# Squares of eleven pairs of heads summed by ScalarE in nine accumulating instructions each, and the order of all work computed anew

## The chip, the cores and the metric

One core of a Trainium2 chip runs the whole program. The metric is the time of one execution in device microseconds, as the median of a few runs; lower is better. One execution was also recorded by the hardware profiler; its trace has the start and the length of every instruction. In what follows PE is TensorE, PEld its weight loads, DVE VectorE, ACT ScalarE, POOL GpSimd and SP the engine that issues most DMAs.

## The reference

Linear attention with random features over 8 batches and 8 heads of 576 rows of 64 numbers, then an MLP (SiLU between two matrices) over the 4608 rows that result:

```python
scale = 1.0 / np.sqrt(np.sqrt(D))
q_s, k_s = (q * scale, k * scale)
def phi(x):
    proj = np.einsum('bhsd,md->bhsm', x, omega)
    sq = np.sum(x * x, axis=-1, keepdims=True) / 2.0
    h = proj - sq
    h = h - np.max(h, axis=-1, keepdims=True)
    return np.exp(h) / np.sqrt(m)
q_p, k_p = (phi(q_s), phi(k_s))
kv = np.einsum('bhsm,bhsd->bhmd', k_p, v)
z = np.sum(k_p, axis=2)
num = np.einsum('bhsm,bhmd->bhsd', q_p, kv)
den = np.einsum('bhsm,bhm->bhs', q_p, z)[..., None] + 1e-06
...
h = x @ w_in
g = h * (1.0 / (1.0 + np.exp(-h)))
return g @ w_out
```

The change is at `sq`, the sum of 64 squares of each row of q and k.

## The kernel before

**Pairs.** Two heads of a batch make a pair; there are 32, numbered 0 to 31, each with a key part (k) and a query part (q). Of each part one copy (`rawk`, `rawq`) comes transposed for PE and one (`nat`) with rows on partitions, 128 by 9 columns by 64, for the squares. `square` squares the `nat` tile on ACT in place, in one instruction of 576 elements a partition; `square_sum` adds 64 squares each on DVE into nine numbers (`sqk`, `sqq`). There are two `nat` buffers for all pairs; a buffer is free for the next load when the sum has read it.

**From a pair to its output.** PE projects (`project`, and `project_mid` for the 128 rows that straddle the two heads, called the middle). DVE takes the maximum of each row (`top`) and makes the shift out of maximum and square sum (`shift`, tiles `nbk` and `nbq`). Then one of two routes: *direct*, where ACT computes nine exponentials straight out of PSUM with the shift as bias (`expo`), or *lowered*, where DVE adds the shift in three operations (`lower`) and ACT takes one exponential over all 1152 columns (`expo_all`). `straight(n, who)` decides: direct below pair 8, and from `STRAIGHT_K` or `STRAIGHT_Q` on. Then PE sums the keys (`zsum`, for the first eight pairs `zsum_direct`) and multiplies them with v (`kv`), DVE makes the normalizer (`denom`: nine or ten products with an accumulator and one reciprocal, tile `rd`), POOL multiplies the queries by it (`normal`), PE transposes them (`turn`; ACT copies, tile `en`) and multiplies (`numer`). ACT copies the result out (`x_high`, `x_rest`), DVE makes its low part (`x_low`).

**The MLP.** The first three blocks of 512 rows go through `stage1` (first matrix, bank h or fx), `silu` and `g_low`, and `stage2` (second matrix, bank acc), with every operand in a high and a low part, so three matmuls stand for one. The other rows go through three rounds of a matrix scheme with seven products in place of eight: `product` and `gather` for the first matrix, `whole_silu`, `g_sum`, `g_high` (ACT) and `g_rest` (DVE, the low part) and `second` for the second. PE starts with the pairs alone; the MLP's first steps come in between from about 58 us on, from about 464 us the scheme's rounds share the time with the last pairs, and from 752 us on PE has the MLP alone.

**What sets the order.** All of it stands in a list of units, each with an engine, a booked length, a due time (`key`), the units that must come before it, and the buffers that it takes and frees. `Plan.run` places them one after the other and so fixes the order on every engine; an engine then works strictly in that order and waits by semaphores for the others. The constants at the head (`STAY`, `SLACK`, `SPREAD_*`, `EARLY_SUMS`, `PREPARE_*`, `LEAD_W`) shift due times; each seed in `SHIFTS` moves the due times of a random part of the units. PSUM has eight banks: four acc, one h, one fx, two att, and the plan decides which bank a unit gets. Before the first projection PE is kept warm by matmuls of `ones` (`warm` and `pulses`).

Of the kernel before, what the change touches and what calls it, by code (L numbers as in the profile page):

```python
# [13 lines left out]
AF = mybir.ActivationFunctionType  # L14
# [5 lines left out]
P = 128  # L20
# [16 lines left out]
DIRECT = 8  # L37
STRAIGHT_K = 22.298
STRAIGHT_Q = 24.404
NARROW = 4  # L40
# [14 lines left out]
for _f in range(16):  # L55
# [19 lines left out]
SWITCH = 1.3  # L75
STAY = 19.856
HANDOFF = {"PE": 0.25, "ACT": 0.1, "DVE": 0.1, "POOL": 0.15, "SP": 0.2}
CALM = 0.5
SHIFTS = (
# [3 lines left out]
)  # L83
# [233 lines left out]
def attention_mlp(ctx: ExitStack, tc: tile.TileContext, qT, kT, qn, kn, v, om_in, w_in, w_out, out, out_t):  # L317
# [55 lines left out]
    def square(n, who):  # L373
        nat = T["nat", n, who]
        nc.scalar.activation(nat, nat, AF.Square, scale=SCALE * 0.5**0.5)  # L375

# [639 lines left out]
    for n in range(NWIN):  # L1016
        calm = n < LEAD
        for i, who in enumerate("kq"):
# [3 lines left out]
            def prev(s):  # L1022
                return [(s,) + x for x in last]
# [566 lines left out]
```

## Time and profile before

| | |
|---|---|
| median of 3 runs | 1021.39 us (1021.1 to 1022.64) |
| profiled execution, its own time | 1022.64 us |
| span of its instructions | 1020.8 us |
| mean granted TensorE clock | 0.990 |
| square on ACT, 64 instructions | 44.3 us |
| sum of squares on DVE, 64 instructions | 2 x 23.8 us |
| first MLP matmul | 58.39 us |
| last pair's last product on PE | 750.59 us |
| last matmul ends | 1016.4 us |

The busy time of PE is modelled at the ends of its matmuls, so a busy PE is not a full one. The slices on the page cut the span in 40 parts of 25.5 us; a digit is the busy share in tenths. Of the page's other parts: the chain of work that ended last is PE for 81%, DVE for 10%, ACT for 4% and DMA for 3%, and DVE's part of it lies between 463 us and 719 us and in the first 100 us.

### The profile page before, as it was taken

The page shows a single profiled execution, that of the slowest core. Times are in us where ns is not written, and L with a number is a line of the kernel's source. Part 1 is how long each engine was busy: PE and PEld are TensorE (multiplying, and loading weights), DVE is VectorE, ACT ScalarE, POOL GpSimd, SP SyncE. Part 2 cuts the span into 40 slices and gives each one's busy share as a digit, 9 for nine tenths or more (in the row PEclk, how much of TensorE's full clock was granted, in tenths as well). Part 3 has the DMA queues.
Part 4 walks back from the last instruction along what each step waited for, and adds up shares of the span by engine and source line. Part 5 has one row for each costly group of instructions (what it writes and reads, how often), then busy time and mean ns, then how long its engine had stood idle before and what let it go on. Part 6 is the DMA issues. An engine that isn't in the chain of part 4 may idle for free.

```text
span 1020.8 us, 17425 instructions
## 1 busy us (share of the span) xinstructions
PE 987.1 (97%) x5792; PEld 792.2 (78%) x5792; DVE 786.1 (77%) x1895; ACT 615.5 (60%) x1225; POOL 359.3 (35%) x447
## 2 busy tenths in 40 slices
PE   7879998999999999999999998999999999999997
PEld 6757877777777787787777776877878888888886
DVE  5879888877877787888986699998657984556863
ACT  4678676655566666676879685656635553324541
POOL 1425554466757776575563313230100000000000
PEclk9889999999999999999999999999999999999999
DMA  7676667677776777768888665866555568566564
GB/s 286 209 254 202 217 239 255 219 248 243 227 227 211 248 243 236 243 226 300 291 282 295 207 198 179 306 211 235 195 200 202 188 209 258 193 197 195 189 213 154
DMA packets 107592, 232.94 MB, mean 228 GB/s; under 512 B 14704, under 2 KB 39408, under 8 KB 107504
## 3 DMA queue, kind: packets, MB, share of 16 engines
q1 hardware_dynamic: 107200, 231.52, 68.2%
q8 instruction: 46, 0.75, 0.3%
q10 hardware_dynamic: 304, 0.33, 0.1%
q14 instruction: 42, 0.34, 0.1%
HBM read 182.52 MB, written 49.28 MB: 227 GB/s over the span
## 4 chain that ended last, share of the span: by engine, by line
PE 81%; DVE 10%; ACT 4%; DMA 3%; issue 1%; POOL 0%; POOLq 0%; SPq 0%; DVEq 0%; ACTq 0%
PE ps_acc L822 13%; PE ps_acc L936 12%; PE ps_acc L983 11%; PE ps_h L737 11%; PE ps_att L936 4%; PE ps_att L822 3%; PE ps_fx L936 3%; PE ps_att L402 3%; DVE prod L488 2%; PE ps_h L936 2%; PE ps_fx L822 2%; PE ps_fx L402 2%; PE ps_fx L500 2%; PE ps_att L500 1%; PE ps_fx L737 1%
## 5 line engine op out<-in xcount | busy, mean ns | idle before, releaser
L822 PE MATMUL ps_acc<-w,x 128*128 128x512 f32 x696 | 171.9, 396 | 0.9 <-DVE w L869 0.5
L822 PEld LDWEIGHTS ps_acc<-w,x 128*128 128x128 f32 x696 | 127.9, 188 | 29.1 <-DVE w L869 0.7
L518 POOL TENSOR_TENSOR hq<-hq,rd 128x384 f32<-128x384 f32 x96 | 82.2, 882 | 188.6 <-DVE rd L493 152.2
L737 PE MATMUL ps_h<-x,w 128*128 128x512 f32 x504 | 133.9, 403 | 3.3 <-ACT en L536 2.6
L983 PE MATMUL ps_acc<-wo,gh 128*128 128x512 f32 x384 | 124.6, 405 | 0.0
L737 PEld LDWEIGHTS ps_h<-x,w 128*128 128x128 f32 x504 | 92.1, 190 | 24.4 <-ACT en L536 2.8
L936 PE MATMUL ps_acc<-w,x 128*128 128x512 f32 x360 | 94.1, 394 | 0.4 <-DVE w L926 0.4
L983 PEld LDWEIGHTS ps_acc<-wo,gh 128*128 128x128 f32 x384 | 67.9, 188 | 14.5
L936 PEld LDWEIGHTS ps_acc<-w,x 128*128 128x128 f32 x360 | 66.6, 188 | 15.2 <-DVE w L926 0.9
L983 PE MATMUL ps_acc<-wo,gl 128*128 128x512 f32 x192 | 75.2, 392 | 0.0
L488 DVE CUSTOM_DVE_ANT_0 prod<-hq,ps_att 128x128 f32<-128x128 f32 (+1 forms) x160 | 45.9, 287 | 26.3 <-PE ps_att L508 12.0
L936 PE MATMUL ps_acc<-gh,x 128*128 128x512 f32 x160 | 58.2, 393 | 0.0
L375 ACT ACTIVATE nat<-nat 128x576 f32<-128x576 f32 x64 | 44.3, 696 | 20.7 <-DMA nat<-qn 10.8
L880 DVE TENSOR_TENSOR gl<-gf,gh 128x512 fp32r<-128x512 f32 x48 | 39.5, 825 | 13.9 <-ACT gf L876 13.7
L874 ACT ACTIVATE gh<-ps_h 128x512 fp32r<-128x512 f32 x42 | 25.1, 598 | 37.1 <-PE ps_h L737 34.6
L459 POOL TENSOR_TENSOR t<-hk 128x256 f32<-128x256 f32 x48 | 38.3, 817 | 22.6 <-ACT hk L452 20.4
L983 PEld LDWEIGHTS ps_acc<-wo,gl 128*128 128x128 f32 x192 | 36.0, 188 | 8.0
L536 ACT COPY en<-ps_att 128x384 f32<-128x384 f32 x46 | 21.7, 480 | 33.8 <-PE ps_att L524 30.7
L936 PEld LDWEIGHTS ps_acc<-gh,x 128*128 128x128 f32 x160 | 30.1, 188 | 6.3
L822 PE MATMUL ps_att<-w,x 128*128 128x512 f32 x138 | 34.8, 390 | 0.0
L779 POOL TENSOR_TENSOR wraw<-w,wraw 128x256 fp32r<-128x256 f32 x32 | 24.3, 758 | 27.9 <-ACT wraw L777 27.3
L467 POOL TENSOR_TENSOR es<-es,hk 64x128 f32<-64x128 f32 x48 | 26.4, 549 | 19.2 <-ACT hk L438 16.6
(450 smaller groups left out, 2534.7 us busy)
## 6 DMA issues: line engine op xcount, KB each, us to landing
x<-ws SPq DMA_DIRECT2D x84, 512.0 KB, 4.3
x<-wt SPq DMA_DIRECT2D x48, 512.0 KB, 4.0
x<-wo_d SPq DMA_DIRECT2D x72, 256.0 KB, 3.3
wo<-wo_d SPq DMA_DIRECT2D x32, 512.0 KB, 3.9
rawk<-kT SPq DMA_DIRECT2D x32, 352.0 KB, 4.0
rawq<-qT SPq DMA_DIRECT2D x32, 352.0 KB, 4.7
v<-v SPq DMA_DIRECT2D x32, 320.0 KB, 4.5
nat<-kn SPq DMA_DIRECT2D x32, 288.0 KB, 4.2
```

The source lines that it names most:

```text
L375: nc.scalar.activation(nat, nat, AF.Square, scale=SCALE * 0.5**0.5)
L402: nc.tensor.matmul(ps[:, i * M : (i + 1) * M], raw[r, o : o + P], oms[r], start=True, stop=True)
L459: nc.gpsimd.tensor_tensor(T["t", n][:, part], e[:, 5 * part : 5 * part + 2], e[:, 5 * part + 2 : 5 * part + 4], ALU.add)
L467: nc.gpsimd.tensor_tensor(T["es", n][r, j], T["es", n][r, j], e[r, MID], ALU.add)
L488: nc.vector.tensor_tensor_reduce(out=prod[r], in0=e[r, c], in1=z[r, j * M : (j + 1) * M], scale=1.0, scalar=GUARD, op0=ALU.mult, op1=ALU.a ...
L500: nc.tensor.matmul(ps[j * D : (j + 1) * D, :M], vt[:, c + j], e[:, c], start=i == 0, stop=i == 4)
L518: nc.gpsimd.tensor_tensor(e[:, c], e[:, c], rd[:, c].unsqueeze(2).broadcast_to([P, 3, M]), ALU.mult)
L737: nc.tensor.matmul(ph, w[:, i], x[:, j], start=k == 0 and n == 0, stop=k == NK - 1 and n == 2)
L822: nc.tensor.matmul(ph, ws[:, u, kk * P : (kk + 1) * P], o[:, x], start=i in (0, 1, 4) and kk == 0 and n == 0, stop=kk == 1 and n == 2, ski ...
L880: nc.vector.tensor_tensor(gl, T.pop(("gf", t, f)), T["gh", t, f].bitcast(F32), ALU.subtract)
L936: nc.tensor.matmul(T["qb", p, chain][d], w[:, u, d * P : (d + 1) * P], x, start=i in (0, 1, 4) and s == 0 and n == 0, stop=s == NS - 1 and ...
L983: nc.tensor.matmul(T["po", t][j], g[:, js], w, start=f == 0 and n == 0, stop=f == NF - 1 and n == 2)
```

## The change

The test `summed(n)` picks pairs 22 to 31 (22.000 is the border) and, by its second half, pair 0. For these ACT squares and sums in one: nine instructions of 64 columns, each with an accumulator output that goes into one of the nine numbers. The DVE reduction of these 22 tiles falls away, and the `nat` buffer is free after ACT's ninth. The borders of the direct route move: k from pair 23 on before, from 26 now; q from pair 25 on before, from 24 now. Constants and seeds (40 before, 48 now) are others, and by them the whole order.

```diff
@@ -35,8 +35,10 @@
+SUMMED_FROM = 22.000
+SUMMED_TO = 0.482
-STRAIGHT_K = 22.298
-STRAIGHT_Q = 24.404
+STRAIGHT_K = 25.339
+STRAIGHT_Q = 23.117
...
-STAY = 19.856
+STAY = 17.388
...
-    55, 761, 1230, 1684, 2043, 2652, 3396, 5453, 5899, 6430, 7010, 8410, 8796, 9966, 11076, 11672, 12487,
+    39, 528, 1932, 2796, 3494, 4104, 5306, 6136, 6388, 6984, 7584, 7818, 8321, 8679, 9726, 10682, 11322,
...
-EARLY_SUMS = 18.806
-PREPARE_1 = 22.764
-PREPARE_2 = 2.035
-LEAD_W = 14.593
+EARLY_SUMS = 14.192
+PREPARE_1 = 16.093
+PREPARE_2 = 12.582
+LEAD_W = 13.938
@@ -372,6 +375,12 @@
         nat = T["nat", n, who]
+        if summed(n):
+            T.pop(("nat", n, who))
+            T["sq", n, who] = s = new(f"sq{who}", [P, 10])
+            for c in range(NC):
+                nc.scalar.activation(nat[:, c], nat[:, c], AF.Square, scale=SCALE * 0.5**0.5, accum_out=s[:, c : c + 1])
+            return
         nc.scalar.activation(nat, nat, AF.Square, scale=SCALE * 0.5**0.5)
@@ -1007,6 +1016,9 @@
+    def summed(n):
+        return n >= SUMMED_FROM or n < SUMMED_TO
...
-                add(("sq",) + w, "ACT", 0.7, at(n, 2 * i - 4, 13 + 10 * i - 32), lambda n=n, who=who: square(n, who),
-                    after=[("nat",) + w])
-                add(("ssum",) + w, "DVE", 0.76, at(n, 2 * i - 3, 14 + 10 * i - 32), lambda n=n, who=who: square_sum(n, who),
...
+                wide = summed(n)
+                add(("ssum",) + w if wide else ("sq",) + w, "ACT", 2.3 if wide else 0.7, at(n, 2 * i - 4, 13 + 10 * i - 32), lambda n=n, who=who: square(n, who),
...
+                if not wide:
+                    add(("ssum",) + w, "DVE", 0.76, at(n, 2 * i - 3, 14 + 10 * i - 32), lambda n=n, who=who: square_sum(n, who),
```

In all, 22 ACT instructions of 576 columns become 198 of 64 columns; ACT has 18 direct exponentials fewer and two of 1152 columns more, and two table loads fewer; DVE has 22 reductions fewer and six `lower` operations more; PE has one warming matmul more. POOL and SP have as many instructions as before.

Lines in the new program are some 9 higher in this part (L379 of before has no counterpart, L418 is L427, L477 is L486, L488 is L497, L926 is L935).

**The start, on DVE.** The first rows of DVE's program, before; `sqk` and `sqq` are pair 0's sums, `mxk` and `mxq` its maxima, `nbk` and `nbq` its shifts.

```order
L379 TENSOR_REDUCE sqk<-nat 128x9
L418 TENSOR_REDUCE mxk<-ps_att 128x4
L418 TENSOR_REDUCE mxk<-ps_fx 128x4
L379 TENSOR_REDUCE sqq<-nat 128x9
L416 TENSOR_REDUCE mxk<-ps_acc 128x1
L422 TENSOR_TENSOR nbk<-mxk,sqk 128x9
L423 SCALAR_TENSOR_TENSOR nbk<-nbk,sqk 128x9
```

And now:

```order
L427 TENSOR_REDUCE mxk<-ps_att 128x4
L427 TENSOR_REDUCE mxk<-ps_fx 128x4
L425 TENSOR_REDUCE mxk<-ps_acc 128x1
L431 TENSOR_TENSOR nbk<-mxk,sqk 128x9
L432 SCALAR_TENSOR_TENSOR nbk<-nbk,sqk 128x9
```

The two reductions are gone; the shift of the keys follows the maxima at once. On PE, 17 warming matmuls stand ahead of the first projection in place of 13, and the three ahead of pair 1's projection are gone. Somewhat later PE runs three groups of `stage1` ahead of pair 3's query projection, which stood ahead of them; on DVE the query shift of pair 3 comes behind the one of pair 4, and the normalizers of pairs 3 and 4 follow each other; on ACT the three copies of pair 2's transposes stand ahead of the squares of pair 4, where the third stood behind them.

**Pair 7's key sum, on PE.** Before, from the query middle of pair 7 (L409) over the second stage (L983), the product with v and the output product of pair 6 (L500, L562) to the key sum (L477, L479) and the next `stage1` step (L737):

```order
L409 MATMUL ps_fx<-oms,rawq 128x128
L983 MATMUL ps_acc<-wo,gh 128x512 x2
L983 MATMUL ps_acc<-wo,gl 128x512
L500 MATMUL ps_att<-hk,v 64x128 x10
L562 MATMUL ps_att<-en,kw 64x512 x2
L562 MATMUL ps_att<-en,kw 64x64 x2
L477 MATMUL ps_fx<-hk,sides 128x128
L479 MATMUL ps_fx<-hk,ones 128x128 x4
```

Now, from the end of the `stage1` step (L746) over the middle (L418) and the key sum (L486, L488) to the second stage (L992):

```order
L533 MATMUL ps_att<-ident,hq 128x128 x3
L746 MATMUL ps_h<-x_1079,w_1867 128x512 x3
L418 MATMUL ps_att<-oms,rawq 128x128
L486 MATMUL ps_fx<-hk,sides 128x128
L488 MATMUL ps_fx<-hk,ones 128x128 x4
L486 MATMUL ps_fx<-hk,sides 128x128
L488 MATMUL ps_fx<-hk,ones 128x128 x4
L992 MATMUL ps_acc<-wo,gh 128x512 x2
```

The middle has moved from bank fx to a bank of att, so the key sum no longer takes the bank that the middle's exponential must free. The product with v and the output product (now L509, L571) come after the key sum and four groups of the second stage.

**Pair 27's normalizer, on DVE.** Before, its last read and its reciprocal (L488, L493) with what follows; L926 is `g_rest`, L902 `g_sum`, L418 to L423 maxima and shift of pair 28:

```order
L488 ISA den 128x1
L493 RECIPROCAL rd<-den 128x9
L902 TENSOR_TENSOR x_6025<-w_7062,x_6025 128x512
L926 TENSOR_TENSOR w_7067<-wo,w_7067 128x512
L418 TENSOR_REDUCE mxk<-ps_att 128x4
L902 TENSOR_TENSOR x_6025<-w_7062,x_6025 128x512
L418 TENSOR_REDUCE mxk<-ps_att 128x4
L422 TENSOR_TENSOR nbk<-mxk,sqk 128x2x4
L423 SCALAR_TENSOR_TENSOR nbk<-nbk,sqk 128x2x4
L926 TENSOR_TENSOR gl<-wo,gh 128x512
```

Now, the same low parts (L935; `w_7186` and the `gl` behind it are the ones that were `w_7067` and `gl` above):

```order
L935 TENSOR_TENSOR w_7186<-wo,w_7186 128x512
L911 TENSOR_TENSOR x_5602<-w_7046,x_5602 128x512
L911 TENSOR_TENSOR w_7244<-wo,w_6784 128x512
L911 TENSOR_TENSOR w_6784<-w_6784,x_6864 128x512
L427 TENSOR_REDUCE mxk<-ps_h 128x4
L431 TENSOR_TENSOR nbk<-mxk,sqk 128x2x4
L432 SCALAR_TENSOR_TENSOR nbk<-nbk,sqk 128x2x4
L911 TENSOR_TENSOR x_5602<-w_7046,x_5602 128x512
L935 TENSOR_TENSOR gl<-wo,gh 128x512
L935 TENSOR_TENSOR w_7206<-wo,w_7206 128x512
```

The normalizer is not among them: it stands 17 rows further on. Pair 27's key sum has moved on PE too, behind the first group of the following product.

More of the change, by code (lines that the diff above doesn't have):

```diff
@@ L92 @@
 STRETCH_0 = 1.362
-SLACK = 0.818
+SLACK = 0.811
 PAIRS_4 = 195.050
@@ L97 @@
 PAIRS_28 = -59.566
-SPREAD_IN = 2.859
-SPREAD_OUT = 10.456
-SPREAD_AT = 366.656
+SPREAD_IN = 2.756
+SPREAD_OUT = 10.080
+SPREAD_AT = 355.349
 SPREAD_LATE = 469.554
-EARLY_SUMS = 18.806
-PREPARE_1 = 22.764
-PREPARE_2 = 2.035
-LEAD_W = 14.593
+EARLY_SUMS = 14.192
+PREPARE_1 = 16.093
+PREPARE_2 = 12.582
+LEAD_W = 13.938
 PREPARE = (PREPARE_1, PREPARE_2)
@@ L1034, in attention_mlp @@
                     order=before, alloc=[("nat", ("nat",) + w)], lat=1.1)
-                add(("sq",) + w, "ACT", 0.7, at(n, 2 * i - 4, 13 + 10 * i - 32), lambda n=n, who=who: square(n, who),
-                    after=[("nat",) + w])
-                add(("ssum",) + w, "DVE", 0.76, at(n, 2 * i - 3, 14 + 10 * i - 32), lambda n=n, who=who: square_sum(n, who),
-                    after=[("sq",) + w], order=[] if n and n - 1 < LEAD and who in WHOLE else prev("ssum"), alloc=[(f"sq{who}", ("ss",) + w)], free=[("nat",) + w])
+                wide = summed(n)
+                add(("ssum",) + w if wide else ("sq",) + w, "ACT", 2.3 if wide else 0.7, at(n, 2 * i - 4, 13 + 10 * i - 32), lambda n=n, who=who: square(n, who),
+                    after=[("nat",) + w], order=prev("ssum") if wide else [], alloc=[(f"sq{who}", ("ss",) + w)] if wide else [], free=[("nat",) + w] if wide else [])
+                if not wide:
+                    add(("ssum",) + w, "DVE", 0.76, at(n, 2 * i - 3, 14 + 10 * i - 32), lambda n=n, who=who: square_sum(n, who),
+                        after=[("sq",) + w], order=[] if n and n - 1 < LEAD and who in WHOLE else prev("ssum"), alloc=[(f"sq{who}", ("ss",) + w)], free=[("nat",) + w])
             o = 6.2 + 10.8 * i
```

5 rows, old and new, of the table SHIFTS are left out of this document.

## The prediction

> **What bounds the kernel now.** I read the busy shares and the slices first, then the table of windows by stage, then the list of what TensorE (PE) waited for, and last the timeline around its longest waits.
>
> ```profile
> PE 987.1 (97%) x5792; PEld 792.2 (78%) x5792; DVE 786.1 (77%) x1895; ACT 615.5 (60%) x1225; POOL 359.3 (35%) x447
> ...
> PEclk9889999999999999999999999999999999999999
> ```
>
> PE is busy for 97% of the span, so a change can win only what PE does not use. Where that is, the windows say (the columns are the stretch, its length, then busy time of PE, PEld, DVE, ACT and POOL with instruction counts, granted clock, DMA share, GB/s):
>
> ```profile
> 0.00:100.00 100.00, 83.22 (x645) 67.27 (x646) 78.61 (x233) 68.27 (x186) 36.10 (x46) 0.91 0.71 237
> ...
> 100.00:150.00 50.00, 49.98 (x300) 40.56 (x298) 41.53 (x102) 35.18 (x70) 25.25 (x26) 1.00 0.69 230
> 150.00:190.00 40.00, 34.98 (x210) 28.35 (x211) 34.85 (x75) 26.65 (x46) 19.38 (x20) 0.96 0.68 229
> 190.00:460.00 270.00, 269.79 (x1744) 213.21 (x1744) 212.85 (x591) 169.79 (x295) 180.15 (x232) 1.00 0.73 237
> 460.00:700.00 240.00, 234.48 (x1486) 184.60 (x1485) 208.68 (x539) 171.20 (x378) 90.62 (x116) 1.00 0.73 250
> ...
> 750.00:1016.00 266.00, 264.50 (x1168) 217.77 (x1167) 171.90 (x264) 114.74 (x194) 0.00 (x0) 1.00 0.62 203
> ```
>
> From 190 to 460 us PE is idle for 0.2 us, from 750 to 1016 for 1.5 us; in both the work of PE alone sets the time, and that work stays (the same matmuls in another order, one warming matmul more). What is to be had lies in three places: 16.8 us idle, at a granted clock of 0.91, in the first 100 us; 5.0 us between 150 and 190; 5.5 us between 460 and 700. The waits in the last two:
>
> ```profile
> PE ps_fx L477 <- ACT hq L438: 2.6, 1, 2.6
> ...
> PE ps_acc L936 <- DVE gl L926: 1.2, 1, 1.2
> ...
> PE ps_h L402 <- DVE den L488: 1.1, 1, 1.1
> ```
>
> The first is one wait at 161 us. The other two stand between 611 and 619 us, in a stretch where VectorE (DVE) is the full engine, while ScalarE (ACT) was fuller before it:
>
> ```profile
> 450.00:600.00 150.00, 147.84 (x946) 115.96 (x945) 123.03 (x339) 118.89 (x239) 73.90 (x100) 1.00 0.78 265
> 600.00:700.00 100.00, 96.63 (x597) 76.63 (x595) 95.41 (x217) 61.72 (x153) 24.16 (x24) 1.00 0.67 226
> ```
>
> DVE is busy for 95% from 600 to 700 us and PE loses 3.4 us there. From 450 to 600 ACT has 79% and DVE 82%.
>
> **The change, part 1: what moves between ACT and DVE.**
>
> ```profile
> L375 ACT ACTIVATE nat<-nat 128x576 f32<-128x576 f32 x64 | 44.3, 696 | 20.7 <-DMA nat<-qn 10.8 <-DMA nat<-kn 7.7 <-DVE den L488 1.1
> ...
> L379 DVE TENSOR_REDUCE sqk<-nat 128x9 f32<-128x576 f32 x32 | 23.8, 744 | 4.9 <-ACT nat L375 4.8
> ...
> 53.06 2.18 ACT L438 ACTIVATE hk<-ps_acc,nbk 128x128 f32<-128x128 f32 x8
> ...
> L438 ACT ACTIVATE hk<-ps_att,nbk 128x128 f32<-128x128 f32 x86 | 24.5, 385 | 6.3 <-DVE nbk L423 6.2
> ...
> L446 DVE TENSOR_TENSOR hk<-ps_att,nbk 128x512 f32<-128x512 f32 x19 | 12.7, 683 | 0.6
> ...
> L443 DVE TENSOR_SCALAR hk<-ps_att,nbk 128x128 f32<-128x128 f32 x15 | 5.3, 351 | 0.6
> ...
> L452 ACT ACTIVATE hk<-hk 128x1152 f32<-128x1152 f32 x15 | 17.5, 1167 | 0.2
> ...
> L438 ACT ACT_TABLE_LOAD x17 | 21.8, 1283 | 3.9 <-DVE nbq L423 1.8 <-DVE nbk L423 1.8
> ```
>
> The test takes pairs 22 to 31 and also pair 0, so 22 tiles lose their DVE reduction: 22 x 0.744 = 16.4 us less DVE. The shifted borders of the direct exponentials turn three key tiles to the DVE route and one query tile away from it, net two more: 2 x (2 x 0.683 + 0.351) = 3.4 us. DVE: -13.0 us.
>
> On ACT a tile goes from one pass of 0.70 us to nine accumulating instructions of 64 columns, which the trace has not. The nearest row is the eight exponentials of 128 columns, (2.18 - 0.385) / 7 = 0.256 us apart, so nine take 2.3 us. Fewer columns speak for less, a read of the accumulator for more; I take 2.3. Below, a tile cannot cost less than the one pass it has now, 0.7; above, nine exponentials with no overlap are 9 x 0.385 = 3.5. So 22 x (2.3 - 0.7) = +35.2 us. Against it stand 18 exponentials fewer (18 x 0.256 = -4.6), two long ones more (+2.3) and two table loads fewer in the new order (-2.6): ACT +30.3 us, to 646 us of the span or 63%. With the ends of the price it is -4.9 and +56.7.
>
> The Trainium skill ("ScalarE: Activation LUTs", What ACT_TABLE_LOAD costs) gives an ACTIVATE with immediate operands 186 ns plus 0.833 ns a column, and 93 ns of overlap back to back. An estimate by it is 9 x 146 + 93 ns = 1.4 us a tile, which lies inside my bounds; it names no price for the accumulator output. The trace agrees where it can: 186 + 480 = 666 ns for 576 columns beside a mean of 696. By this price the ACT term of the sum below would be 0, and the forecast 1015.4.
>
> Where ACT's extra work lands:
>
> ```profile
> 450.00:600.00 150.00, 9.34 (x14) 1.00 0.78 265
> ```
>
> This is the square alone in that window: 14 of the tiles. ACT there becomes 118.9 + 14 x 1.6 - 4.9 = 136.4 of 150 us, 91%. What is queued behind a long sum on ACT is what PE waits for: copies of transposes, exponentials, the copies out of the products. They have slack now (none of the named waits between 460 and 700 us over 0.6 us is ACT's), but at 91% some of it goes. I charge **+1.0**. Something also comes back: a tile's buffer is now free after ACT's own sum, not after DVE's place in its queue, so the reload is issued earlier; 18.5 us of the square's idle time in the row above ended at such loads.
>
> **Part 2: the start.** Four edits act on the first 100 us.
>
> ```profile
> 3.78 4.19 PE L351 MATMUL ps_att<-ones 128*128 128x128 f32 x26
> ...
> 10.30 0.75 DVE L379 TENSOR_REDUCE sqq<-nat 128x9 f32<-128x576 f32 x1
> ...
> 56.57 1.41 ACT L375 ACTIVATE nat<-nat 128x576 f32<-128x576 f32 x2 [1.33 <-DMA nat<-qn]
> ...
> 57.88 0.46 ACT L536 COPY en<-ps_h 128x384 f32<-128x384 f32 x1
> ...
> 67.47 0.29 DVE L488 CUSTOM_DVE_ANT_0 prod<-hq,ps_acc 128x128 f32<-128x128 f32 x1 [0.20 <-PE ps_acc L479]
> ```
>
> Pair 0's query sum (0.75 us) stood between two maxima on DVE, ahead of the first shift, and goes: -0.75. But 17 warming matmuls stand ahead of the first projection in place of 13. The 13 (26 records) took 4.19 us, 0.32 each, so four more cost 1.3 at most; the later ones come closer together, and I take 1.0. The two nearly cancel. The third transpose of pair 0 gets a bank of its own and pair 1's key shift moves ahead of its query maxima, which the exponentials behind them use up again: no more than 0.5 by 55 us. Then the last copy of pair 2's transposes (57.88) no longer stands behind the load of pair 4's query tile, for which PE waits 2.6 us now:
>
> ```profile
> PE ps_h L737 <- ACT en L536: 2.6, 1, 2.6
> ```
>
> That -2.6 is given back: PE now runs three of the first MLP matmul groups before pair 3's query projection, the third of them needs a copy that ACT makes behind pair 4's two loads, and DVE brings pair 3's query shift last instead of first. Counted along DVE's new order with about 0.7 us an operation, pair 3's normalizer starts 4 us after its 67.47, and the two normalizers then run one behind the other. With the cover of the work moved ahead, the first MLP step ends later by 1 to 2 us. Start in all: **+1.0**, with -3 and +6 as ends.
>
> **Part 3: the wait at 161 us.**
>
> ```profile
> 159.44 1.28 ACT L874 ACT_TABLE_LOAD   x1
> ...
> 161.84 1.28 ACT L438 ACT_TABLE_LOAD   x1
> ...
> 163.14 0.37 ACT L438 ACTIVATE hq<-ps_fx,nbq 128x128 f32<-128x128 f32 x1
> ...
> 163.56 0.79 PE L477 MATMUL ps_fx<-hk,sides 128*128 128x128 f32 x2 [2.55 <-ACT hq L438]
> ...
> 159.70:163.14 3.44, 1.30 (x15) 0.60 (x10) 3.40 (x5) 3.40 (x5) 1.85 (x2) 1.00 0.71 249
> 163.14:166.55 3.41, 2.99 (x14) 3.00 (x15) 2.38 (x5) 2.63 (x7) 0.00 (x0) 0.50 0.93 284
> ```
>
> Pair 7's denominator sum needs bank fx, which held its query middle; that exponential came behind a SiLU and two table loads. In the new order the middle is in att and fx is free after an earlier exponential, so the 2.55 us go. So does most of the half clock behind it: 3.41 us at 0.50 cost 1.7. What is late next is the key-value product behind it, which needs the att bank that the same exponential frees, again behind a SiLU with two loads (163.51 - 159.44 = 4.1 us, with one step between and the hand-overs some 5). PE has the sum, some 2 us at full clock, and four second-stage groups, 2.72, to do meanwhile:
>
> ```profile
> 170.24 2.72 PE ps_acc L983 x12
> ```
>
> I leave 1 us of wait, and of the 1.7 take 1.5: 2.55 + 1.5 - 1.0 = 3.0, so **-3.0**, with 0 and -4.2 as ends.
>
> The Trainium skill ("TensorE: Matmul & The Clock Gate", Part 1: The HAM clock gate) has the clock halved after at least one idle window of about 3.4 us. The rows differ: PE was busy for 1.30 of the 3.44 us ahead of the half clock. By the page a 2.55 us wait would not halve the clock, the 1.5 us would not come back with it, and the forecast would be 1017.9.
>
> **Part 4: 460 to 700 us.**
>
> ```profile
> 610.80 0.28 DVE L488 CUSTOM_DVE_ANT_0 prod<-hq,ps_h 128x128 f32<-128x128 f32 x1
> ...
> 614.14 0.22 DVE L493 RECIPROCAL rd<-den 128x9 f32<-128x9 f32 x1
> ...
> 614.82 1.32 DVE L926 TENSOR_TENSOR w<-wo,w 128x512 fp32r<-128x512 f32 x1
> ```
>
> Pair 27's normalizer holds DVE from 610.80 to 614.36, and the low part that PE's next second-stage group wants comes behind it. Of PE's waits here 1.1 + 1.2 stand in the rows above. In the new order the six low parts of that stage that came behind the normalizer run ahead of it, and the sums of pairs 28 to 31 have left DVE. I take the whole 3.4 us that PE idles from 600 to 700 less 0.4: **-3.0**. Elsewhere in the stretch PE waits for DVE twice more:
>
> ```profile
> PE ps_fx L822 <- DVE wraw L869: 0.6, 1, 0.6
> ...
> PE ps_acc L822 <- DVE w L869: 0.5, 1, 0.5
> ```
>
> These give **-1.0**. Ends for both: +1 and -6, since pairs 24 to 30 now stand later among the matmuls and press on what follows.
>
> **The sum.** +1.0 - 3.0 - 3.0 - 1.0 + 1.0 = -5.0 us. The span of 1020.8 becomes 1015.8 and the profiled execution's 1022.64 becomes 1017.6. The median of the runs, 1021.39, is 1.25 below that execution: **1016.4**.
>
> **Rivals.** 0.2%, or 2 us, is about what a measurement of this kernel can tell from no change.
>
> *The start eats it.* The load of pair 4's tiles now stands ahead of work that PE wants next. At the end +6 of the start's term the sum is 0: 1021.4. For it: ACT already waits at that load. Against it: PE has work of four pairs there.
>
> *ScalarE becomes the bound between 450 and 600 us.* This ends on the other side. DVE at 95% cost PE 3.4 us in 100; ACT reaches 95% of 150 us (142.5) when a tile costs 0.7 + (142.5 - 118.9 + 4.9) / 14 = 2.7 us. At 3.5 us ACT has 118.9 - 4.9 + 14 x 2.8 = 153.2 of 150: 3.2 over and 5.1 for the waits, 8.3 in place of 1.0, and the -1.0 of that stretch is lost: 1024.7. For it: DVE's accumulating instructions (L488) each have a second record that reads the accumulator. Against it: eight exponentials overlap well.
>
> *More than that.* If ACT's term and the start's come to 0 and the other DVE stretches (PE's 5.5 us of idle and its pipeline restarts around them) give 3 us more, it is 1011.4.
>
> **How the numbers follow.** The forecast, 1013 to 1019, has 0.48; more than that 0.17; the start eats it 0.18; ScalarE bound 0.17. Faster by over 0.2%: 0.65; within: 0.18; slower: 0.17. The range 1009 to 1024 takes in the first three and the near end of ScalarE's.
>
> **What would show it.** Nine records of about 0.25 us, or nine and nine reads, for each summed tile; DVE near 773 us and ACT near 646; the wait of L486 on an exponential near 160 us gone and the clock at 1.0 there; no wait on DVE's L935 around 615 us; PE idle from 190 and from 750 us on as it is. Wrong is the step on ACT if its share from 450 to 600 us passes 95%, and the start if pair 3's normalizer begins after 74 us.

## The result and the profile after

The changed kernel takes **1031.23 us** (median of 4 runs, 1029.52 to 1031.68) beside 1021.78 us for before on the same chip. The ratio is 1.0094, with a 95% interval of 1.008 to 1.0108: slower by some 9.5 us, where 5 us less were forecast. The profiled execution took 1031.14 us with a span of 1029.3; before's span was 1020.8, so 8.5 us are to be found in the two traces.

The busy times and the granted clock on the page of after:

```profile
PE 989.2 (96%) x5794; PEld 791.5 (77%) x5794; DVE 780.3 (76%) x1879; ACT 643.9 (63%) x1581; POOL 364.6 (35%) x447
...
PEclk9898999999999999999999999999999999999999
```

PE does the same work. ScalarE (ACT) is busy for 28.4 us more, where 30.3 were forecast, and VectorE (DVE) for only 5.8 us less, where 13.0 were. The windows of after, in the columns of the prediction:

```profile
0.00:100.00 100.00, 79.78 (x623) 64.27 (x624) 77.71 (x230) 68.08 (x213) 35.51 (x46) 0.90 0.71 235
...
150.00:190.00 40.00, 34.04 (x211) 26.73 (x210) 35.01 (x71) 25.82 (x49) 20.27 (x19) 0.99 0.60 193
190.00:460.00 270.00, 270.00 (x1734) 214.17 (x1734) 211.21 (x582) 167.47 (x309) 179.67 (x229) 1.00 0.73 236
460.00:700.00 240.00, 232.43 (x1447) 181.50 (x1446) 198.80 (x526) 192.36 (x678) 90.52 (x115) 1.00 0.75 245
...
450.00:600.00 150.00, 147.64 (x967) 115.85 (x966) 113.40 (x333) 125.48 (x445) 72.24 (x97) 1.00 0.77 254
600.00:700.00 100.00, 94.79 (x541) 73.83 (x540) 94.73 (x211) 72.81 (x257) 22.30 (x24) 1.00 0.69 224
```

From 450 to 600 us, where 14 of the sums run, PE lost nothing (147.64 us busy beside 147.84), though ACT went up from 118.89 to 125.48. PE lost 3.4 us of busy time in the first 100 us, 0.9 between 150 and 190, 1.8 between 600 and 700. What PE waited for, longest first:

```profile
PE ps_fx L418 <- DVE hk L455: 3.4, 1, 3.4
PE ps_fx L746 <- ACT x L590: 2.9, 2, 2.3
PE ps_fx L533 <- DVE sqq L388: 2.6, 1, 2.6
PE ps_acc L533 <- POOL hq L527: 2.4, 1, 2.4
PE ps_fx L746 <- DVE den L497: 2.0, 1, 2.0
PE ps_h L411 <- DVE den L497: 1.9, 1, 1.9
```

None of these is a wait for a sum on ACT. The third, which ends at 38.7 us, is put down to a sum of squares that stayed on DVE, of an early pair; before waits for 3.3 us at the same transposes, put down to a shift on DVE. The first ends at 187.6 us, the last at 694.8 us, and the others lie between 47 and 85 us. The sum itself, in the groups of ACT:

```profile
L382 ACT ACTIVATE nat<-nat 128x64 f32<-128x64 f32 x198 | 47.8, 258 | 1.0 <-DVE nbk L432 0.9
L382 ACT ACTIVATION_READ_ACCUMULATOR nat<-nat 128x1 f32 x198 | 39.7, 203 | 0.0
L384 ACT ACTIVATE nat<-nat 128x576 f32<-128x576 f32 x42 | 29.2, 704 | 14.9 <-DMA nat<-qn 12.1 <-DMA nat<-kn 2.6
```

There are nine records and nine reads for a tile. They overlap; from first start to last end a tile takes 2.27 us (mean of the 22).

**The lag.** A time that a kernel loses is not where PE waits longest, because the wait may have stood there before. So I found every unit of PE's work (a projection, a product, a stage) in both traces, added up their lengths in the kernel's own order at one fixed length per kind, and compared the times at which the two kernels have done the same amount. The difference is the lag, positive where a kernel is behind before. Its rows here are named by before's time. Two executions with the same order and the same operations up to 420 us (two experiments below) differ by 2 us in it from the start on, so a difference of 1 or 2 us that is there by 65 us says nothing. The traced execution of before took 0.9 us more than the median of its four, so the lags are about that much too low beside the medians.

| before's us | after | sums alone | order alone | sums twice | start to 210 | late four | both | after's start |
|---|---|---|---|---|---|---|---|---|
| 63.6 | -3.2 | -1.5 | -2.4 | 0.4 | -1.1 | -2.9 | -1.9 | -3.0 |
| 110.6 | 3.5 | -1.6 | 3.5 | 6.9 | -1.2 | 3.6 | -2.1 | 4.2 |
| 173.9 | -0.3 | -2.1 | -0.4 | 3.0 | -1.6 | -0.3 | -3.7 | 3.8 |
| 196.9 | 4.9 | -1.3 | 4.9 | 8.3 | -1.5 | 5.0 | -2.9 | 3.8 |
| 419.6 | 4.0 | -1.5 | 4.0 | 7.5 | -1.6 | 4.1 | -3.1 | 4.3 |
| 602.7 | 4.9 | 13.6 | 8.9 | 28.9 | -0.6 | 5.0 | -2.1 | 4.7 |
| 638.6 | 3.0 | 13.6 | 7.3 | 27.2 | -2.7 | 3.0 | -4.2 | 4.7 |
| 679.8 | 5.7 | 14.2 | 10.1 | 35.2 | 0.1 | 4.6 | -2.7 | 4.7 |
| 753.6 | 8.6 | 14.0 | 13.4 | 38.8 | 2.9 | 4.9 | -2.3 | 4.8 |

The column of after has three losses: 6.7 us between 64 and 111 us, 5.2 between 174 and 197, 5.6 between 639 and 754 (5.3 of them at 671 to 705 us of its own trace). It has two gains, 3.8 between 111 and 174 and 1.9 between 603 and 639. In between it is flat, over all the sums from 420 to 600 us too.

**The start.** On the timeline of after, pair 3's denominator begins here on DVE, and POOL and PE follow (start, length, engine, line, and in brackets what ended the idle time):

```profile
70.77 1.66 DVE L675 SCALAR_TENSOR_TENSOR w<-wraw,w 128x512 uint32<-128x512 uint32 x1
72.36 0.28 DVE L497 CUSTOM_DVE_ANT_0 prod<-hq,ps_acc 128x128 f32<-128x128 f32 x1
```

```profile
76.90 2.40 POOL L527 TENSOR_TENSOR hq<-hq,rd 128x384 f32<-128x384 f32 x3 [2.44 <-DVE den L497]
```

```profile
77.78 0.90 PE L533 MATMUL ps_acc<-ident,hq 128*128 128x128 f32 x3 [2.43 <-POOL hq L527]
```

The denominator stands behind four weight steps (the L671 and L675 kind), begins 4.9 us later than before's, and PE waits for what follows from it. The waits are only half of the loss. From 76.2 to 83.0 us PE runs at half clock, which before does not at this place (columns of the windows, the clock third from the end; first after, then before):

```profile
75.00:80.00 5.00, 2.55 (x11) 1.93 (x11) 4.21 (x31) 1.50 (x5) 2.40 (x3) 0.62 0.92 353
80.00:85.00 5.00, 4.27 (x27) 2.55 (x25) 3.45 (x9) 1.79 (x7) 2.40 (x3) 0.70 0.22 67
```

```profile
75.00:80.00 5.00, 3.74 (x33) 2.44 (x33) 4.63 (x21) 3.38 (x11) 2.07 (x3) 1.00 0.13 24
80.00:85.00 5.00, 4.51 (x31) 3.36 (x31) 4.86 (x9) 4.20 (x12) 3.12 (x4) 1.00 0.44 152
```

The half clock costs 5 x 0.38 + 5 x 0.30 = 3.4 us. From 65 to 90 us PE is idle for 6.6 us in after and for 2.9 in before, which makes the other half. The traces of all the kernels below that keep after's order through this stretch show the same half clock there.

**At 184 us.** PE, then the DVE instructions that stand ahead of the one it waits for:

```profile
187.56 0.46 PE L418 MATMUL ps_fx<-oms,rawk 128*128 128x128 f32 x2 [3.44 <-DVE hk L455]
```

```profile
179.50 1.67 DVE L671 SCALAR_TENSOR_TENSOR w<-wre,w 128x512 uint32<-128x512 uint32 x1
181.20 1.20 DVE L675 SCALAR_TENSOR_TENSOR w<-wraw,w 128x512 uint32<-128x512 uint32 x1
...
186.72 0.69 DVE L455 TENSOR_TENSOR hk<-ps_fx,nbk 128x512 f32<-128x512 f32 x1
```

DVE has no gap over 0.3 us from 172.8 to 188 us. Bank fx, which the middle of pair 8's keys wants, comes free only when DVE has come to L455. The granted clock is then 0.50 from 188.8 to 192.2 us, 1.7 us more: with the wait of 3.4 us that is the 5.2 us of the lag.

### The profile page after: what moved, and what is told of

Its sections match the earlier page's. It is cut to its first block, busy times and chain, and to the rows that moved or that the text cites. A ratio compares the mean times of both kernels' runs of the same rounds, so it can differ in the third digit from the quotient of the medians.

```text
span 1029.3 us, 17764 instructions
## 1 busy us (share of the span) xinstructions
PE 989.2 (96%) x5794; PEld 791.5 (77%) x5794; DVE 780.3 (76%) x1879; ACT 643.9 (63%) x1581; POOL 364.6 (35%) x447
## 4 chain that ended last, share of the span: by engine, by line
PE 82%; DVE 9%; ACT 4%; DMA 2%; issue 2%; POOL 1%; POOLq 0%; SPq 0%; DVEq 0%; ACTq 0%
PE ps_acc L831 14%; PE ps_acc L992 12%; PE ps_acc L945 12%; PE ps_h L746 9%; PE ps_att L945 5%; PE ps_att L411 4%; PE ps_att L831 3%; PE ps_fx L746 3%; PE ps_h L945 2%; PE ps_att L509 2%; DVE prod L497 2%; PE ps_h L831 2%; PE ps_att L571 1%; PE ps_fx L831 1%; PE ps_att L533 1%
## 5 line engine op out<-in xcount | busy, mean ns | idle before, releaser
L831 PE MATMUL ps_acc<-w,x 128*128 128x512 f32 x726 | 178.7, 395 | 0.0
L831 PEld LDWEIGHTS ps_acc<-w,x 128*128 128x128 f32 x726 | 133.4, 188 | 28.7
L527 POOL TENSOR_TENSOR hq<-hq,rd 128x384 f32<-128x384 f32 x96 | 86.3, 924 | 165.7 <-DVE rd L502 123.1
L992 PE MATMUL ps_acc<-wo,gh 128*128 128x512 f32 x384 | 124.4, 405 | 0.0
L746 PE MATMUL ps_h<-x,w 128*128 128x512 f32 x456 | 120.7, 401 | 0.6 <-ACT gf L885 0.6
L746 PEld LDWEIGHTS ps_h<-x,w 128*128 128x128 f32 x456 | 82.3, 188 | 18.8 <-POOL w L692 0.6
L945 PE MATMUL ps_acc<-w,x 128*128 128x512 f32 x357 | 93.4, 394 | 1.3 <-DVE w L935 1.3
L992 PEld LDWEIGHTS ps_acc<-wo,gh 128*128 128x128 f32 x384 | 69.0, 190 | 14.0
L945 PEld LDWEIGHTS ps_acc<-w,x 128*128 128x128 f32 x357 | 66.0, 188 | 16.5 <-DVE w L935 2.4
L992 PE MATMUL ps_acc<-wo,gl 128*128 128x512 f32 x192 | 75.5, 393 | 0.0
L382 ACT ACTIVATE nat<-nat 128x64 f32<-128x64 f32 x198 | 47.8, 258 | 1.0 <-DVE nbk L432 0.9
L497 DVE CUSTOM_DVE_ANT_0 prod<-hq,ps_att 128x128 f32<-128x128 f32 (+1 forms) x120 | 34.4, 287 | 16.1 <-ACT kw L522 5.7
L992 PEld LDWEIGHTS ps_acc<-wo,gl 128*128 128x128 f32 x192 | 36.3, 189 | 8.1
L497 DVE CUSTOM_DVE_ANT_0 prod<-hq,ps_fx 128x128 f32<-128x128 f32 (+1 forms) x110 | 31.5, 287 | 13.3 <-ACT kw L522 5.9
L545 ACT COPY en<-ps_att 128x384 f32<-128x384 f32 x44 | 21.1, 484 | 29.9 <-PE ps_att L533 27.2
L382 ACT ACTIVATION_READ_ACCUMULATOR nat<-nat 128x1 f32 x198 | 39.7, 203 | 0.0
L384 ACT ACTIVATE nat<-nat 128x576 f32<-128x576 f32 x42 | 29.2, 704 | 14.9 <-DMA nat<-qn 12.1
```

Of the source, the lines that this page charges most:

```text
L382: nc.scalar.activation(nat[:, c], nat[:, c], AF.Square, scale=SCALE * 0.5**0.5, accum_out=s[:, c : c + 1])
L497: nc.vector.tensor_tensor_reduce(out=prod[r], in0=e[r, c], in1=z[r, j * M : (j + 1) * M], scale=1.0, scalar=GUARD, op0=ALU.mult, op1=ALU.a ...
L527: nc.gpsimd.tensor_tensor(e[:, c], e[:, c], rd[:, c].unsqueeze(2).broadcast_to([P, 3, M]), ALU.mult)
L746: nc.tensor.matmul(ph, w[:, i], x[:, j], start=k == 0 and n == 0, stop=k == NK - 1 and n == 2)
L831: nc.tensor.matmul(ph, ws[:, u, kk * P : (kk + 1) * P], o[:, x], start=i in (0, 1, 4) and kk == 0 and n == 0, stop=kk == 1 and n == 2, ski ...
L945: nc.tensor.matmul(T["qb", p, chain][d], w[:, u, d * P : (d + 1) * P], x, start=i in (0, 1, 4) and s == 0 and n == 0, stop=s == NS - 1 and ...
```

## The experiments

Fifteen kernels. Those that move units do it with a small helper that takes the planned order and puts a unit directly behind another one of its engine, keeping every dependence and buffer; only its list is shown. "Before's order up to T" means that each engine works off the units that it had begun by T us in a trace of before's order with ScalarE's sums, in that order and with those banks, and then the rest in after's; T is called the seam. After's order includes its routes (direct or lowered), which the kernels with before's order do not have.

**1. The sums alone, in before's order (sums alone).**

```diff
     def square(n, who):
...
+        if n >= 22 or n == 0:
...
+            T["sq", n, who] = s = ring.tile([P, 10], F32, tag=f"wide{who}", name=f"wide{who}", bufs=4)
+            for c in range(NC):
+                nc.scalar.activation(nat[:, c], nat[:, c], AF.Square, scale=SCALE * 0.5**0.5, accum_out=s[:, c : c + 1])
+            return
         nc.scalar.activation(nat, nat, AF.Square, scale=SCALE * 0.5**0.5)
...
     def square_sum(n, who):
+        if ("nat", n, who) not in T:
+            return
```

> The order of before, with the sums of pairs 0 and 22 to 31 made by nine accumulating ScalarE instructions where the one square stood; VectorE's reductions of these tiles are gone; the sums get four buffers of their own so that the order can stay. Theory 1 (the sums cost what the trace shows, 2.27 us a tile, and all of it is hidden; the loss is in the new order): within 2 us of before, 1020 to 1024 us, ScalarE busy near 645 us and no wait of TensorE over 1.5 us that before does not have. Rival (the longer blocks on ScalarE make the loss wherever they stand): 1028 us or more, with the lag growing between 430 and 690 us.

Measured: 1035.07 us, ratio 1.0132 (1.0114 to 1.0149). Theory 1 falls, and the rival's place is right for this order: the lag goes from -1.5 to +13.6 us between 420 and 593 us and nowhere else. Its window from 450 to 600 us and PE's waits in it:

```profile
450.00:600.00 150.00, 139.77 (x875) 108.73 (x874) 100.44 (x304) 127.30 (x458) 68.49 (x95) 0.97 0.75 248
```

```profile
PE ps_att L417 <- ACT hq L446: 2.6, 1, 2.6
PE ps_fx L410 <- ACT hk L446: 1.8, 1, 1.8
PE ps_fx L516 <- ACT kt L513: 1.6, 1, 1.6
```

PE is busy for 8.1 us less than before and has a clock of 0.97, though ACT is only at 127.3 of 150 us, 85%. These waits are for exponentials and a copy that ACT comes to only behind a sum and a table load. ACT in after has nearly the same share there (84%) and costs PE nothing, so a share does not tell what the sums cost; what they stand in front of does.

**2. The order alone (order alone).** After's order, square and reduction as in before, the reduction on DVE at most eight units behind the square, and earlier where a load or a shift comes first. The planner did not place these reductions.

```diff
-            for c in range(NC):
-                nc.scalar.activation(nat[:, c], nat[:, c], AF.Square, scale=SCALE * 0.5**0.5, accum_out=s[:, c : c + 1])
+            nc.scalar.activation(nat, nat, AF.Square, scale=SCALE * 0.5**0.5)
+            held.append([nat, s, 0])
...
+            sum_held(u["name"])
```

> The order of after, but the tiles of pairs 0 and 22 to 31 are squared by one ScalarE instruction and summed by one VectorE reduction a few units later, as before did it. Theory 1 (the new order loses): the time of after, 1029 to 1033 us, with the lag curve of after (+6.7 us between 60 and 93 us, +4.1 near 183, +5.3 between 671 and 705). Rival (the sums on ScalarE lose): the time of before, 1020 to 1024 us.

Measured: 1037.72 us, 1.016 (1.0145 to 1.0175), above what either theory gave. From 111 to 420 us the lag is after's to a tenth of a microsecond, so what is lost there is the order's and not the late sums'. Behind them it falls a further 4.8 us behind after: in the new order the sums on ACT are a gain over reductions put there by hand. The two halves of the change are each slower alone (13.6 and 16.2 us) than together (9.5).

**3. The sums twice (sums twice).**

```diff
+            for c in range(NC):
+                nc.scalar.activation(nat[:, c], nat[:, c], AF.Square, scale=SCALE * 0.5**0.5, accum_out=spare[:, c : c + 1])
```

> After, with each of the nine accumulating instructions given twice (the second time into a spare tile that nobody reads, on values already squared): 20 tiles by 2.27 us, about 45 us more on ScalarE, which was busy 192.4 of 240 us between 460 and 700 us and would be busy near 233. Theory 1 (ScalarE has the room, the order makes the loss): at most 5 us over after, 1031 to 1036 us. Rival (ScalarE's blocks set the time): at least as much again as the change lost, 1040 us or more.

Measured: 1062.14 us, 1.0402 (1.0384 to 1.042), the rival's number. Of the 30 us by which its lag ends over after's, some 20 come between 420 and 603 us. ACT is busy for 44.1 us more than in after (688.0), and 31 of them come out as time: it does not have a second 2.3 us a tile free.

**4. Three places moved by hand.**

```diff
+        (('top', 3, 'q', 2), ('top', 3, 'q', 1)),
+        (('nb', 3, 'q', 0), ('top', 3, 'q', 2)),
+        (('exp', 3, 'q', 2), ('exp', 4, 'k', 2)),
...
+        (('den', 3), ('nb', 4, 'q', 2)),
+        (('wd', 'out', 13, 0), ('low', 8, 'k', 1)),
...
+        (('ol', 1, 1, 0), ('qU3', 0, 1)),
+        (('ol', 1, 0, 0), ('qC22', 0, 1)),
+        (('den', 29), ('ql', 0, 6, 5)),
+        (('proj', 31, 'k'), ('m2', 0, 6, 5)),
```

> After, with three places of the order changed and all sums left on ScalarE: pair 3's query shift and exponentials ahead of pair 4's and its denominator ahead of the weight steps (start), three weight steps of tile 13 behind the low parts of pair 8's keys (183 us), and the operand sums of the next round and the denominator of pair 29 later (671 to 705 us). Theory 1 (these places make the loss): 4 + 3.5 + 3 to 5 us back, 1018 to 1022 us. Rival (the sums on ScalarE): 1028 us or more.

Measured: 1034.69 us, 1.0131 (1.0116 to 1.0146), 3.5 us worse than after. By the lag the first group made the start worse (5.4 at 111 us, where after has 3.5), 174 to 197 us, the place of the second, became worse (+11.4 in place of +5.2), and only at the place of the last did it gain: from 639 to 754 us it loses 1.9 where after loses 5.6.

**5. The last group alone (late four).** The last four lines of the list above.

> After, with four moves in the last third alone: the operand sums ol 1 1 0 and ol 1 0 0 behind qU3 and qC22, the denominator of pair 29 behind ql 0 6 5, the projection of pair 31's keys behind m2 0 6 5. If VectorE's place in the order makes the 5.3 us between 671 and 705 us: 3 to 5 us back, 1026 to 1028.5 us. Rival (ScalarE's sums of pairs 29 to 31 make it): 1030 us or more.

Measured: 1028.47 us, 1.0074 (1.0062 to 1.0087), at the upper edge of what VectorE's place would give; the rival falls, as the sums are where they were. The windows of before, of after and of this kernel there:

```profile
660.00:715.00 55.00, 54.91 (x318) 44.06 (x317) 50.36 (x121) 31.69 (x74) 10.22 (x11) 1.00 0.68 224
```

```profile
660.00:715.00 55.00, 51.10 (x299) 39.84 (x298) 50.57 (x118) 35.34 (x108) 15.81 (x16) 1.00 0.64 211
```

```profile
660.00:715.00 55.00, 54.04 (x316) 42.62 (x315) 51.09 (x131) 38.87 (x117) 15.39 (x16) 1.00 0.70 228
```

DVE is as full in all three (92, 92 and 93%); PE gets 2.9 us back, and DVE now does first what PE wants first. Three of the four moves are DVE's and one is a projection on PE; what each gives was not tried. By the ratios it is 2.0 us (1.0094 less 1.0074), about as much as the two intervals leave open; the traced execution took 0.8 us less than the median, so the 3.7 us of its lag are a little much. With the start repaired as well (experiments 7 and 8) the same moves give 4.7 us (1.0039 less 0.9993).

**6 and 7. Before's order at the start.** Up to 105 us, and up to 210 us (start to 210).

```diff
-        for u in plan.run():
+        for u in rearranged(plan.run(), first, moves):
```

> After, but every engine first works off what it did in before's order up to 105 us (the sum of pair 0 on ScalarE at the place of its square), and then goes on in after's order. If the start makes +4.0 us of the loss (lag at 110 us of work +4.0 in after, -1.6 in the run with before's order and the sums), 5.6 us come back: 1024.5 to 1027 us. Rival (what the start loses is lost a little later in any case, as the hand-made moves of the last run suggest): 1029 us or more.

Measured: 1031.45 us, 1.0105 (1.0089 to 1.0121): nothing gained, the rival's number. Up to 105 us the lag is -1.6; at the seam PE then waits once for 4.3 us, for a bank that an exponential of ACT's frees (ps_att L517 <- ACT hk L447), and the lag is after's again.

> As the run before, but with before's order up to 210 us. In before's order the wait at 161 us (3.0 us) comes back and the loss at 176 to 190 us (4.9 us) goes, so the lag at 200 us should be near -1.4 us and the end 4.6 us (what after loses from there) later: 1023.5 to 1026 us. If the loss between 671 and 705 us depends on what stands at the start, the end differs by more than 2 us from this.

Measured: 1025.34 us, 1.0039 (1.0027 to 1.0052), as expected. The lag is -1.5 at 197 us and then runs beside after's, 5.5 to 6.4 us below it, to the end. So the order of the first 210 us carries 5.6 us of the loss (1.0094 less 1.0039), and what comes behind does not depend on it.

**8. Both repairs (both).**

> After with both repairs: before's order up to 210 us, and the four moves in the last third. The first gave 1025.34 us and the second 1028.47 us, against 1031.2 us for after. If the two losses stand by themselves: 1031.2 - 5.9 - 2.8 to 3.7, which is 1021.5 to 1022.5 us, the time of before, with all twenty late sums still on ScalarE. Rival (one place hands its loss to the other): 1024 us or more.

Measured: 1020.94 us (12 runs), 0.9993 (0.9984 to 1.0002). With the sums of all 22 tiles still on ScalarE the time is that of before. Its windows:

```profile
0.00:100.00 100.00, 85.21 (x662) 69.36 (x663) 79.53 (x233) 73.42 (x222) 37.49 (x48) 0.91 0.73 242
150.00:190.00 40.00, 35.33 (x210) 28.14 (x209) 35.49 (x77) 24.92 (x45) 19.05 (x19) 1.00 0.69 236
...
600.00:700.00 100.00, 97.23 (x562) 75.95 (x562) 95.69 (x218) 72.34 (x256) 24.98 (x26) 1.00 0.74 238
```

PE has 5.4, 1.3 and 2.4 us more in them than in after. The whole loss is in the order of these stretches. (Of its lag, -2.3, some 1.7 us are a half clock at 162 us that the kernel of experiment 7 has with the same order there and this execution has not; the ratio is the better number.)

**9. After's start in before's order (after's start).** The other way round: after's units up to 105 us of its trace, then before's order, with the late sums on DVE.

> Before's order, but every engine first works off what it did in after's order up to 105 us (sum of pair 0 on ScalarE; the late sums stay one square and one reduction). This asks whether after's late start is paid at the end, or taken up by the wait at 161 us that before's order has anyway. If that wait takes it up: lag near +4 us at 110 us of work, near +1 behind 161 us of trace, and an end at 1021.5 to 1023 us. If the start is paid in full: 1025 us or more.

Measured: 1027.12 us, 1.006 (1.0045 to 1.0075). The start is paid in full: the lag is 4.2 at 111 us and 3.8 at 174, since before's order still waits at 161 us, only later, and 4.8 at the end.

**10. The wait at 161 us taken out of before.**

```diff
+        (('exp', 7, 'q', 2), ('re', 'in', 12)),
```

> Before, with one unit moved: ScalarE's exponential of the middle block of pair 7's query (exp 7 q 2) ahead of silu 0 10 instead of behind it. At 161 us of before TensorE waits 2.55 us for it; ScalarE reaches it only at 163.14 us because the silu and two idle stretches of 1.31 us stand ahead of it, while its input (nb 7 q 2) is there at 160.60 us. If that is the whole wait: 2 to 2.5 us gained, 1018.7 to 1019.5 us. Rival (VectorE is behind in this stretch and the wait comes back by 190 us): 1020.5 to 1022 us.

Measured: 1021.23 us (12 runs), 1.0003 (0.9993 to 1.0013): no gain. The wait is gone and the lag -3.7 at 174 us, but -0.1 at 197. The windows of the traced execution show what took it back there (the clock stands third from the end):

```profile
178.00:179.70 1.70, 1.70 (x12) 1.34 (x10) 1.70 (x3) 0.79 (x2) 1.62 (x2) 1.00 0.22 88
179.70:181.40 1.70, 1.04 (x7) 0.60 (x5) 1.53 (x6) 1.38 (x4) 0.08 (x1) 1.00 0.70 202
181.40:183.10 1.70, 0.81 (x7) 0.74 (x8) 1.70 (x5) 1.68 (x3) 0.00 (x0) 0.75 0.04 15
183.10:184.80 1.70, 1.70 (x13) 1.48 (x10) 1.63 (x4) 1.51 (x2) 0.00 (x0) 0.50 0.49 43
184.80:186.50 1.70, 1.70 (x5) 1.31 (x5) 1.70 (x3) 0.20 (x1) 1.00 (x2) 0.50 0.92 369
186.50:188.20 1.70, 1.70 (x5) 1.31 (x5) 1.60 (x4) 0.48 (x1) 1.62 (x3) 0.50 0.98 331
188.20:189.90 1.70, 1.70 (x7) 1.33 (x7) 1.42 (x3) 0.00 (x0) 1.10 (x1) 0.74 1.04 411
```

DVE is full here (11.28 of 11.9 us), and PE waits in two short pieces:

```profile
180.54 0.52 PE L524 MATMUL ps_fx<-ident,hq 128*128 128x128 f32 x3 [0.66 <-ACT en L536]
...
182.36 2.07 PE L402 MATMUL ps_att<-oms,rawq 64*128 64x128 f32 x14 [0.89 <-DVE hk L443]
```

Then the clock halves: 1.7 x (0.25 + 3 x 0.50 + 0.26) = 3.4 us. The rival was right on the time; of its cause one of the two waits is VectorE's. This is one execution, and it took 2.0 us more than the median of the twelve. Over all twelve the granted clock is 0.988 in the mean where before's is 0.990, which is some 1.3 us; what took back the rest in the others is not shown.

**11. The same move with both repairs.**

> The first kernel of this group with the move of exp 7 q 2 as well. If all three stand by themselves: 1019 to 1020 us, faster than before and after. Rival as in the run before: 1021 us or more.

Measured: 1020.28 us (12 runs), 0.9988 (0.9977 to 0.9999): the fastest of all, by less than the 0.2% that this measurement can tell. Here the clock stays at 1.00 from 150 to 190 us, and 1.0 us of the move is kept (lag at 197 us -3.9, where the kernel without the move has -2.9), which is less than two executions of one order can differ by.

**12. Pair 0's sum and the denominator of pair 27, in before's order.**

```diff
+        (('den', 27), ('ql', 0, 2, 6)),
```

> Before's order, with two things of the change alone: the sum of pair 0 by nine accumulating ScalarE instructions (worth 1.6 us in the run with all sums) and the denominator of pair 27 behind the low parts ql 0 2 0 to ql 0 2 6. If both gains stand by themselves: 1016 to 1019 us, faster than before. Rival (the denominator only hands its wait on): 1019.5 to 1021 us.

Measured: 1029.13 us, 1.0074 (1.006 to 1.0088). Neither expectation. PE's longest wait in this kernel:

```profile
PE ps_h L410 <- DVE den L496: 8.1, 1, 8.1
```

The denominator reads pair 27's sums out of bank h, and the projection of pair 28's query is the next to want that bank. Moved behind five low parts it holds up the projection 8.1 us, and the products that want these low parts stand behind the projection on PE. The new order moved PE's units as well, and in the kernels of the table that have it there the lag falls by 1.6 to 2.1 us between 603 and 639 us. Pair 0's sum shows no gain here (lag +0.7 at 111 us, where the run with all sums had -1.6 with the same order): it can't be told from nothing.

**13 to 15. Where in the start.** One unit alone, and before's order up to 45 and up to 75 us.

```diff
+        (('den', 3), ('nb', 4, 'q', 2)),
```

> After, with one unit moved: the denominator of pair 3 (den 3) directly behind nb 4 q 2, ahead of four weight steps (wd) that stand before it on VectorE. It could start at 68.8 us in place of 72.4, the normalizer of pair 3 at 73 in place of 76.9. If this unit's place makes the start's loss: the 2.4 us wait ahead of the first transpose of pair 3 goes, 1028 to 1029.3 us. Rival (the weight steps then hold up their own readers, so the wait only changes its name): 1030.5 us or more.

Measured: 1034.12 us, 1.0122 (1.0108 to 1.0136), 2.9 us worse than after. The denominator begins at 71.0 us, and the weight steps behind it end 6.7 us later than in after. ScalarE's next pass over a raw weight (L655) comes only at 79.68 us, 4.89 us idle, and stands ahead of the copy that PE's next transpose needs:

```profile
PE ps_acc L517 <- ACT kt L514: 5.0, 1, 5.0
```

> After, with before's order up to 45 us. If the loss of the start is made in after's order behind 60 us (pair 3's chain), nothing changes: lag near +4 us at 110 us of work, 1030 to 1032 us. If what is done ahead of 45 us makes it: lag near -1 to -2, 1025 to 1027 us.

Measured: 1030.46 us, 1.0089 (1.0074 to 1.0105); lag 3.7 at 111 us. The loss is not laid down ahead of 45 us.

> After, with before's order up to 75 us, so that pair 3's query shift, exponentials and denominator stand as in before and the rest as in after. If pair 3's place makes the loss of the start: lag near -1 at 65 us of work, and 1025.5 to 1027.5 us at the end unless a new wait comes behind 75 us. If the loss is made by what follows 75 us: lag near +3 to +4, 1030 us or more.

Measured: 1034.29 us, 1.0126 (1.0113 to 1.014). Up to 75 us the lag is -1.5, and it is 6.9 at 111 us: the seam costs 8.4 us. With the seam at 75 or at 105 us it costs at least as much as what it was to save, so these two say little about after itself.

## Why the prediction was wrong

The sum was +1.0 (start) - 3.0 (161 us) - 3.0 - 1.0 (460 to 700 us) + 1.0 (ScalarE) = -5.0; measured on the trace it is +8.5. By the lag the stretches give +3.5 to 111 us, +1.4 to 197, -0.9 to 420 and +4.6 from there to 754 us. The start lies inside its ends (-3 and +6); the wait at 161 us with what follows it (ends -4.2 and 0) and 460 to 700 us (ends -6 and +1) do not.

- **ScalarE, +1.0: right in size, wrong in what it hung on.** A tile costs 2.27 us, where 2.3 was taken; ACT has 643.9 us (646 forecast), DVE 780.3 (773 forecast; the second and third instruction of the weight steps, the same in number, account for 4.3 of the difference, 54.3 us where before had 50.0). From 450 to 600 us PE lost 0.2 us, and ACT is at 84% there, not at the 91% of the forecast: the sums take 31.6 us of it as counted, but other work of ACT's has left the stretch. The rival "ScalarE becomes the bound" was given its point of decision by a share, 95%. Experiment 1 lost 15 us at 85%. The Trainium skill ("ScalarE: Activation LUTs", What ACT_TABLE_LOAD costs) led to an estimate of 1.4 us a tile, which the trace does not bear out: each accumulating instruction has a second record, the read, of 203 ns.
- **The start, +1.0: this step failed first.** The lag of after is +3.5 at 111 us, and in before's order this start alone costs 6.1 us (ratio 1.006). The step had counted rightly that pair 3's normalizer begins 4 us later (4.9, at 72.36 us; the sign of being wrong that it named, a begin behind 74 us, did not show although the step was wrong) and then let other work cover all but 1 to 2 us of that. The cover was not there, as PE waits 2.43 us for that very normalizer, and the half clock that came with the waits, 3.4 us, was no term of the sum. The 2.6 us wait ahead of it did go (lag -3.2 at 64 us), and what that gave is lost twice over.
- **The wait at 161 us, -3.0: right, and then lost again.** The wait is gone, the clock is 1.00 from 160 to 175 us and the lag falls by some 3 us there. But the step asked what is late next on PE and not who else is full: DVE has 87% of 150 to 190 us in before and 88% in after. The gain is gone by 192 us, in after as one wait of 3.44 us and 1.7 us of half clock, in the trace of experiment 10 as a half clock of 3.4 us. The term is +1.4, not -3.
- **460 to 700 us, -4.0: half right, and one stretch was missed.** In the order that has the low parts ahead of pair 27's normalizer the lag falls by 1.6 to 2.1 us, of the 3.0. But the prediction looked only at the places where before waits. Between 660 and 715 us before had no wait that its list shows (PE busy for 54.91 of 55 us, DVE for 50.36), and after loses 5.3: the low parts of two operand sums of the next round and the denominator of pair 29 now stand ahead of what PE wants. Moving four units gave 2 to 4.7 us of it back.
- **The sum itself** added the work that moves and the new order as terms that stand by themselves. They do not: each part of the change alone loses more (13.6 and 16.2 us) than both (9.5), and repairing the order alone brings the time back to before's. What is then left of the relief of DVE by the sums is too small to be told from nothing (0.9984 to 1.0002).

**What stays open.** Which unit of the first 105 us makes the loss. Pair 3's chain is where PE waits, but putting its denominator first moved the wait to the weight steps (experiment 13), and seams inside this stretch brought new waits, the longest of 4.0 and 4.3 us. Which of the four moves of experiment 5 is needed is open too, and so is what takes back the gain at 161 us in executions that were not traced. The start looks like a DVE with no slack in which something is always last, but that is argued and not shown.

## What to carry to other kernels

When an order is computed anew, the waits of the old trace are only half the list: walk the new order through every stretch where another engine than the bound one is nearly full (here VectorE at 87 to 93%), and ask there which of its pieces now stands in front of something that the bound engine wants, even if nothing waited there before. A wait that is removed inside a stretch where another engine is full can come back within that stretch, as a wait or as a lower clock, as it did in after and in the trace of experiment 10; do not count it in full unless that engine has less to do too. Price a new wait with the half clock that may come with it (here 1.7 to 3.4 us), not by its length alone. And test a change of work and a change of order apart: moved alone, either can lose what both together gain, so a part's worth in one order is not its worth in another.

## What was not expected of the hardware

- **Half clock without a long idle piece.** In experiment 10 the clock fell to 0.50 at 182.3 us, for 6.8 us. In the 3.42 us ahead of that PE was busy for 1.97, and its longest single wait was 0.89 us. The Trainium skill ("TensorE: Matmul & The Clock Gate", Part 1: The HAM clock gate) has it halve after at least one idle window of some 3.4 us; the rows show that less idle time, in pieces, can be enough. It need not be: in experiment 11 PE was busy for 1.85 of the 3.40 us from 177.80 to 181.20 us, and the clock stayed at 1.00.
- **Weight steps of twice their length.** The second instruction of a weight step (L671, 128x512) takes 693 ns in the median and 1.67 us at 179.50 us, when POOL works on tiles as well. That POOL is the cause was not tried.
